# Seven block products instead of eight in the first halves of batches 3, 5 and 7, with the sums of the weight blocks placed anew

## The chip, the cores and the metric

The kernel runs on one core of one Trainium2 chip. The metric is the device time of one execution in microseconds (us). The core has five engines: TensorE (in the profile PE, with its weight loads as PEld), VectorE (DVE), ScalarE (ACT), GpSimd (POOL) and SyncE (SP), which here only starts DMAs. SBUF and PSUM are the core's two on-chip memories; in this kernel the products are written to PSUM, and VectorE and ScalarE read them there.

## The reference

```python
# attention between tokens x (8, 8, 512, 64) and states (8, 8, 32, 64)
xread = softmax(scale * x @ state.T) @ state         # per batch and head
sread = softmax(scale * state @ x.T) @ x
x = concat([xread, sread], axis=2)                   # -> (8 * 544, 512)
# mixture layer: w_in (512, 2048), w_out (2048, 512)
h = x @ w_in
return (h * cos(h)) @ w_out
```

All of it is float32. The kernel folds `state @ w_in` into a small matrix `sw` per batch, so that the first layer of a batch is a product with 256 rows to sum over (2048 x 256 by 256 x 512). It is made in 16 tiles of 128 x 512.

## The kernel before

A batch is 16 tiles. Two batches make a pair, and the second layer of a pair is made by Strassen's seven products already. So the 32 tiles of a pair fall into four phases of eight tiles: 0 and 1 are the two halves of the even batch, 2 and 3 those of the odd one. In phases 2 and 3 the gates are also subtracted from each other (`minus`).

The first layer of a tile is either plain, or it is made for two tiles together by Strassen's products. Plain is two matmuls of 512 columns a tile, four for two tiles. Strassen takes the 2 x 2 blocks of two tiles and needs seven products of 256 columns in place of eight:

```python
def hidden(t):                                   # plain: PE writes one of two PSUM buffers
    t.hp = hps.tile([P, S], F32, name="h")[:, 0:t.n]
    for i in range(t.kn):
        nc.tensor.matmul(out=t.hp, lhsT=t.lhs(i), rhs=t.rhs(i), ...)

def seven(t):                                    # which tiles go through seven products
    return t.pair is not None and t.b > 1 and t.phase < 2

def halves(b): ...    # four differences of 128 x 256 on VectorE, once a batch
def sw_sums(t):       # four sums of 128 x 128 weight blocks, once for two tiles
    ...
        nc.gpsimd.tensor_tensor(o, x1, x2, op=op)
def hidden_a(t, t2): ...   # four of the seven products, one copy on ScalarE
def sums_a(t): ...         # three sums on VectorE
def hidden_b(t): ...       # the other three products
def sums_b(t): ...         # two sums on VectorE
```

After that comes the gate h * cos(h), tile by tile, in four steps that alternate between ScalarE and VectorE:

```python
def gate(t):   nc.scalar.activation(t.q.bitcast(I32), t.hp, func=Copy, bias=0.25)
def gate2(t):  nc.vector.tensor_tensor(t.q, t.q.bitcast(I32), t.hp, op=subtract)
def gate3(t):  nc.scalar.activation(t.q, t.q, func=Sin, bias=halfpi, scale=-TWO_PI)
def gate4(t):  nc.vector.tensor_tensor(t.g, t.hp, t.q, op=mult)   # frees the PSUM buffer
```

Beside the tiles of a batch, the attention of the next batch is worked off by a plan of steps (one step is one tile, counted from 0, so step 8 is the ninth tile). In batches 3 and 5 it puts the scores into step 5 and the maxima, spreads, differences, exponentials, sums and the normalization into steps 5 to 9, most of them on VectorE. Finished results wait in a list (`later`), from which each step takes one: a total or a transpose on VectorE, with the store that follows it.

```python
        gate3(t)
        ...
        if later:
            later.pop(0)()
        for u in all_tiles[step + 3:step + 4]:       # sums for the first tiles of a pair
            if seven(u) and new_pair(u):
                sw_sums(u)
        gate4(t)
        ...
        if step in block_at:
            blocks(*block_at[step])                  # sums of w_out's blocks on GpSimd, once
        for u in all_tiles[step + 2:step + 3]:       # sums for the other tiles
            if seven(u) and u.f % 2 == 0 and not new_pair(u):
                sw_sums(u)
```

## Time and profile before

| | before |
|---|---|
| time, median | 769.69 us (768.45 to 770.36, 4 runs) |
| PE busy | 755.9 us, 98% of the span |
| DVE busy | 487.4 us, 63% |
| ACT, POOL busy | 314.1 us, 227.7 us |
| first layer, plain | 80 tiles |
| first layer, seven products | 24 pairs of tiles |

The prediction shows the lines. One note on reading them: an engine's share in the chain of work tells who was waited for, which is not the same as who was busy.

```profile
311.58 0.65 DVE L578 TENSOR_TENSOR g_all<-h,q 128x512 f32<-128x512 f32 x1
...
312.47 1.02 PE L471 MATMUL h<-aT,sw 128*128 128x512 f32 x2
```

### The profile page before, as it was taken

The page shows a single profiled execution, that of the slowest core. Times are in us where ns is not written, and L with a number is a line of the kernel's source. Part 1 is how long each engine was busy: PE and PEld are TensorE (multiplying, and loading weights), DVE is VectorE, ACT ScalarE, POOL GpSimd, SP SyncE. Part 2 cuts the span into 40 slices and gives each one's busy share as a digit, 9 for nine tenths or more (in the row PEclk, how much of TensorE's full clock was granted, in tenths as well). Part 3 has the DMA queues.
Part 4 walks back from the last instruction along what each step waited for, and adds up shares of the span by engine and source line. Part 5 has one row for each costly group of instructions (what it writes and reads, how often), then busy time and mean ns, then how long its engine had stood idle before and what let it go on. Part 6 is the DMA issues. An engine that isn't in the chain of part 4 may idle for free.

```text
span 768.0 us, 8094 instructions
## 1 busy us (share of the span) xinstructions
PE 755.9 (98%) x2808; PEld 367.0 (48%) x2808; DVE 487.4 (63%) x786; ACT 314.1 (41%) x511; POOL 227.7 (30%) x214
## 2 busy tenths in 40 slices
PE   8998999999999999999999999999999999999997
PEld 3443443444555434445555434455555444455554
DVE  5768777836896558847886558747876546431431
ACT  3887844532353325333362335333443333212112
POOL 2353278776120000653220001751210006500200
PEclk9999999999999999999999999999999999999999
DMA  8596461050012510340105210420100115000021
GB/s 246 170 275 212 127 95 28 7 104 1 10 18 45 93 28 0 55 84 0 27 2 98 41 27 15 76 47 0 28 1 14 22 21 137 0 1 14 15 41 41
DMA packets 161961, 43.52 MB, mean 57 GB/s; under 512 B 153921, under 2 KB 153921, under 8 KB 161921
## 3 DMA queue, kind: packets, MB, share of 16 engines
q1 hardware_dynamic: 161024, 42.49, 25.6%
q10 hardware_dynamic: 768, 0.39, 0.2%
q8 instruction: 22, 0.36, 0.2%
q0 software_dynamic: 128, 0.13, 0.1%
q14 instruction: 19, 0.15, 0.1%
HBM read 34.08 MB, written 8.91 MB: 56 GB/s over the span
## 4 chain that ended last, share of the span: by engine, by line
PE 91%; DVE 3%; POOL 2%; ACT 2%; DMA 1%; issue 1%; ACTq 0%; DVEq 0%; POOLq 0%
PE o L622 49%; PE h L471 20%; PE h L512 9%; PE at L319 4%; PE o L742 4%; PE at L409 2%; PE o L319 1%; POOL g_all L584 1%; PE at L392 1%; DMA g_all<-in_moe_w_in_dram 1%; DMA s<-in_state_dram 0%; POOL w_out L910 0%; DVE q L568 0%; ACT q L565 0%; DVE i L333 0%
## 5 line engine op out<-in xcount | busy, mean ns | idle before, releaser
L622 PE MATMUL o<-g_all,w_out 128*128 128x512 f32 x512 | 236.3, 598 | 0.4 <-POOL w_out L242 0.4
L584 POOL TENSOR_TENSOR g_all<-g_all 128x512 f32<-128x512 f32 x80 | 112.8, 1432 | 241.2 <-DVE g_all L578 241.2
L622 PE MATMUL o<-g_all,s 128*128 128x512 f32 x384 | 177.3, 598 | 0.0
L471 PE MATMUL h<-aT,sw 128*128 128x512 f32 x320 | 152.4, 599 | 2.9 <-DVE g_all L578 2.4
L568 DVE TENSOR_TENSOR q<-q,h 128x512 f32<-128x512 int32 (+1 forms) x93 | 59.4, 639 | 148.7 <-ACT q L565 148.6
L622 PEld LDWEIGHTS o<-g_all,w_out 128*128 128x128 f32 x512 | 93.8, 190 | 118.4 <-issue 114.6
L571 ACT ACTIVATE q<-q,halfpi 128x512 f32<-128x512 f32 (+1 forms) x144 | 100.7, 700 | 86.1 <-DVE q L568 85.9
L565 ACT ACTIVATE q<-h 128x512 int32<-128x512 f32 (+1 forms) x93 | 52.0, 559 | 204.3 <-PE h L471 204.1
L622 PEld LDWEIGHTS o<-g_all,s 128*128 128x128 f32 x384 | 70.8, 190 | 88.5 <-issue 86.5
L471 PEld LDWEIGHTS h<-aT,sw 128*128 128x128 f32 x320 | 60.7, 191 | 80.1 <-issue 67.3
L578 DVE TENSOR_TENSOR g_all<-h,q 128x512 f32<-128x512 f32 (+1 forms) x93 | 59.3, 637 | 35.0 <-ACT q L571 34.6
L565 ACT ACTIVATE q<-g_all 128x512 int32<-128x512 f32 x51 | 31.8, 624 | 90.9 <-DVE g_all L558 90.5
L568 DVE TENSOR_TENSOR q<-q,g_all 128x512 f32<-128x512 int32 x51 | 36.6, 717 | 28.6 <-ACT q L565 28.6
L242 POOL TENSOR_TENSOR w_out<-w_out,s 128x1024 int32<-128x1024 int32 x10 | 23.9, 2391 | 77.7 <-DVE w_out L237 71.5
L578 DVE TENSOR_TENSOR g_all<-g_all,q 128x512 f32<-128x512 f32 x51 | 37.0, 726 | 10.5 <-ACT q L571 10.4
L507 POOL TENSOR_TENSOR swS<-sw 128x128 f32<-128x128 f32 x24 | 11.4, 474 | 84.1 <-PE h L512 66.1
L584 DVE TENSOR_TENSOR g_all<-g_all 128x512 f32<-128x512 f32 x48 | 33.5, 697 | 1.6
L445 ACT COPY sw<-at 128x512 f32<-128x512 f32 x50 | 26.7, 586 | 10.8 <-PE at L319 10.4
L471 PE MATMUL h<-st_all,w_in 128*128 128x256 f32 x128 | 30.2, 379 | 0.0
L242 POOL TENSOR_TENSOR w_in<-w_in,s 128x1024 int32<-128x1024 int32 (+1 forms) x10 | 19.3, 1932 | 36.8 <-DVE w_in L237 34.6
L512 PE MATMUL h<-aS,swS 128*128 128x256 f32 x96 | 28.7, 380 | 1.0 <-POOL swS L507 1.0
L742 PE MATMUL o<-w_out,g_all 128*128 128x512 f32 x64 | 29.6, 592 | 0.0
(103 smaller groups left out, 785.3 us busy)
## 6 DMA issues: line engine op xcount, KB each, us to landing
out_dram<-ot SPq DMA_DIRECT2D x132, 64.0 KB, 2.0
g_all<-in_moe_w_out_dram SPq DMA_DIRECT2D x8, 1024.0 KB, 5.0
g_all<-in_moe_w_in_dram SPq DMA_DIRECT2D x6, 1024.0 KB, 5.4
xT<-in_x_dram SPq DMA_DIRECT2D x96, 64.0 KB, 2.3
x_b<-in_x_dram SPq DMA_DIRECT2D x24, 256.0 KB, 4.4
x_b<-in_x_dram SPq DMA_DIRECT2D x16, 128.0 KB, 3.9
g_all<-in_moe_w_in_dram SPq DMA_DIRECT2D x4, 512.0 KB, 5.8
x_b<-in_moe_w_out_dram SPq DMA_DIRECT2D x1, 1024.0 KB, 6.1
```

What stands on the lines that cost most here:

```text
L242: nc.gpsimd.tensor_tensor(bits, bits, e, op=ALU.add)
L319: nc.tensor.matmul(out=(to or at)[j][Ns * k:Ns * k + Ns, 0:n], lhsT=w[D * j:D * j + D, self.b, Ns * k:Ns * k + Ns], rhs=r(slice(D * j, D * ...
L445: (copy or nc.scalar.copy)(sw_of[self.b, nt][:, j, c0:c1], to[j][:, 0:c1 - c0])
L471: nc.tensor.matmul(out=t.hp, lhsT=t.lhs(i), rhs=t.rhs(i), start=(i == 0), stop=(i == t.kn - 1))
L512: nc.tensor.matmul(out=out, lhsT=w, rhs=r, start=True, stop=True)
L565: nc.scalar.activation(t.q.bitcast(I32), t.hp, func=ACTF.Copy, bias=0.25)
L568: nc.vector.tensor_tensor(t.q, t.q.bitcast(I32), t.hp, op=ALU.subtract)
L571: nc.scalar.activation(t.q, t.q, func=ACTF.Sin, bias=halfpi, scale=-TWO_PI)
L578: nc.vector.tensor_tensor(t.g, t.hp, t.q, op=ALU.mult)
L584: engine.tensor_tensor(out, a, b, op=ALU.subtract)
L622: nc.tensor.matmul(out=acc[bank][ch], lhsT=w[:, i, P * ch:P * ch + P], rhs=g.g, start=(i == 0), stop=(i == NH - 1))
L742: nc.tensor.matmul(out=acc[MAIN][i], lhsT=t.g[:, P * i:P * i + P], rhs=w_out[:, :, t.f, :], start=(t.n_th == 0), stop=(t.n_th == NF - 1))
```

## The change

It aims at TensorE: twelve more pairs of tiles go through seven products instead of eight. The sums of the weight blocks move forward in GpSimd's queue, and those for the very first pair go to VectorE. This is the whole diff, without the lines around it:

```diff
     def seven(t):
-        return t.pair is not None and t.b > 1 and t.phase < 2
+        return t.pair is not None and t.b > 1 and t.phase < 3
@@ sw_sums
+        engine = nc.vector if t.b < 2 or t.b == 2 and t.f == 0 else nc.gpsimd
         for o, x1, x2, op in (...):
-            nc.gpsimd.tensor_tensor(o, x1, x2, op=op)
+            engine.tensor_tensor(o, x1, x2, op=op)
@@ in each step, ahead of gate4
-        for u in all_tiles[step + 3:step + 4]:
-            if seven(u) and new_pair(u):
+        for u, new in zip(all_tiles[step + 2:step + 4], (False, True)):
+            if seven(u) and u.f % 2 == 0 and new_pair(u) == new:
                 sw_sums(u)
@@ in each step, behind the blocks of w_out
-        for u in all_tiles[step + 2:step + 3]:
-            if seven(u) and u.f % 2 == 0 and not new_pair(u):
-                sw_sums(u)
```

## The prediction

> **What bounds the kernel now.** I read the page first: the busy times of the engines, then the chain of work that ended last.
>
> ```profile
> span 768.0 us, 8094 instructions
> PE 755.9 (98%) x2808; PEld 367.0 (48%) x2808; DVE 487.4 (63%) x786; ACT 314.1 (41%) x511; POOL 227.7 (30%) x214
> ...
> PE 91%; DVE 3%; POOL 2%; ACT 2%; DMA 1%; issue 1%; ACTq 0%; DVEq 0%; POOLq 0%
> ```
>
> TensorE is busy for 98% of the span and makes 91% of the chain. The granted clock is 0.998. So a TensorE cycle that is saved is saved in the time, unless another engine then makes TensorE wait. Next come the groups by line, with the shapes apart, for the two ways of computing the first layer. L471 is the plain product. L512 is the Strassen product on half-width blocks.
>
> ```profile
> L471 PE MATMUL h<-aT,sw 128*128 128x512 f32 x320 | 152.4, 599 | 2.9 <-DVE g_all L578 2.4 <-ACT sw L445 0.5
> L512 PE MATMUL h<-aS,sw 128*128 128x256 f32 x96 | 28.9, 382 | 0.5 <-POOL sw L507 0.2 <-ACT g_all L955 0.2
> L512 PE MATMUL h<-aS,swS 128*128 128x256 f32 x96 | 28.7, 380 | 1.0 <-POOL swS L507 1.0
> L512 PE MATMUL h<-aT,sw 128*128 128x256 f32 x96 | 28.5, 379 | 0.0
> L512 PE MATMUL h<-aT,swS 128*128 128x256 f32 x48 | 14.7, 388 | 0.0
> ```
>
> Two things are to be seen. Every matmul in the source is two records: L471 has 320 records for 80 plain tiles with two matmuls each. L512 has 96+96+96+48 = 336 records for 24 pairs of tiles with seven matmuls each. And the mean durations (599 and 380 ns) contain the pipeline's depth, so they don't give the cost. The cost is the distance from one start to the next. I take it from the timeline and the chain: eight records of 512 columns stand there as 3.43 us, so 0.429 us each, and eight records of 256 columns as 1.73 us, so 0.216 us each.
>
> ```profile
> 350.02 1.73 PE h L512 x8
> 351.75 3.43 PE o L622 x8
> ```
>
> The third view is the busy time in stretches. The first line runs from the last Strassen products of batch 2 to the seventh tile of batch 3, so it is the first half of batch 3 less a tile. The second line is the rest of that batch. Columns: time, then busy time of PE, weight loads, DVE, ACT, POOL.
>
> ```profile
> 251.68:293.21 41.53, 41.53 (x139) 17.08 (x137) 24.49 (x38) 13.43 (x23) 0.00 (x0) 1.00 0.29 50
> 293.21:336.73 43.52, 43.52 (x162) 19.28 (x160) 32.57 (x51) 19.51 (x31) 20.05 (x17) 1.00 0.36 61
> ```
>
> In the stretch that the change converts, TensorE is full, VectorE is at 24.49 of 41.53 us and GpSimd does nothing at all. There is room for the sums there.
>
> **What the Trainium skill says.** "FP8 and Floating Point Precision", TensorE Precision Notes: true FP32 takes four passes through the array. "TensorE: Matmul & The Clock Gate", Back-to-back issue gap: a pass of N columns takes about N/2.4 + 2.5 ns, so 216 ns for 512 and 109 ns for 256. The trace agrees: two records of 429 ns are four passes of 215 ns, and two of 216 ns are four of 108 ns. Halving the width therefore costs almost nothing in efficiency, and 7/8 of the products is 7/8 of the time. "SBUF — State Buffer", Who interferes with whom: a DVE instruction with two SBUF inputs contends with a GpSimd instruction that reads SBUF, and the later one blocks. The trace agrees: L493, the differences of the halves, takes 411 ns at best but means of 1015 and 1074 ns where GpSimd's 1.43 us subtractions run beside it, and the sums of the weight blocks (L507) take 450 ns at best and up to 989 ns. The page on TensorE also has, under "Architectural detail", that GpSimd keeps strict order. That is what makes the place of the sums in its queue matter.
>
> **The change, part by part.**
>
> *(a) Products.* The first halves of batches 3, 5 and 7 are 3 x 8 tiles, so 12 pairs. A pair costs 8 records of 512 columns now, 8 x 0.429 = 3.43 us, and then 14 records of 256 columns, 14 x 0.2155 = 3.02 us. That is 0.42 us a pair and, times 12, -5.0 us, all of it on TensorE, the engine that sets the end. TensorE's records go from 2808 to 2808 - 12 x 2 = 2784.
>
> *(b) Sums on VectorE.* A pair adds three sums of 256 columns (415 to 421 ns, L542, L543, L557) and two of 512 (686 and 684 ns, L544, L558): 2.62 us; the gates then read SBUF instead of PSUM (717 to 726 against 682 to 684 ns), 0.04 x 4 = 0.15 us. Twelve pairs: +33 us of VectorE. Each odd batch adds four differences of halves (L493), at 0.41 us if GpSimd is quiet and up to 1 us if not: 1.7 to 4 us, three times. In the stretch shown, VectorE rises from 24.5 to 24.5 + 4 x 2.77 + about 2 = 37.6 us, of 41.5 - 1.7 = 39.8 us. That is 95%, but these stretches are run with three tiles of lag between the gate and the second layer, and the steps where VectorE has most (transposes, maxima) are followed by light ones.
>
> *(c) Copies and block sums.* ScalarE: 12 copies at 0.37 us = 4.4 us, on an engine that is 41% busy. GpSimd: 12 x 4 block sums at 0.45 us = 22 us, where it was idle. Both lie beside TensorE's work. The sums of a pair can start when the products of the pair before have been read, and have a step of about 5 us for 1.8 to 2.5 us of work.
>
> *(d) The sums placed anew.* Where batch 2 begins, GpSimd is late in the kernel before:
>
> ```profile
> 177.60 2.86 POOL L910 TENSOR_TENSOR w_out<-w_out 128x1024 f32<-128x1024 f32 x1
> ...
> 180.43 0.90 POOL L507 TENSOR_TENSOR swS<-sw 128x128 f32<-128x128 f32 x1
> ...
> 182.24 0.70 PE L512 MATMUL h<-aS,swS 128*128 128x256 f32 x2 [1.02 <-POOL swS L507]
> ...
> 183.18 0.70 PE L512 MATMUL h<-aS,sw 128*128 128x256 f32 x2 [0.24 <-POOL sw L507]
> ```
>
> The block subtraction of the second layer's weights (L910, 2.86 us) stands in the queue ahead of the sums for the second pair, and TensorE waits for them. From that pair's first product to the next group of products take 187.58 - 180.63 = 6.95 us here, and 355.02 - 349.86 = 5.16 us at the same place of batch 4, where no such subtraction runs: 1.8 us lost. After the change the sums stand before it, can start at 177.6 and end at about 179.6, before the products at 180.6. I count 1.6 us won, since batch 4 still shows 0.2 us of such a wait. The four sums for the first tile of batch 2 go to VectorE: 4 x about 0.3 us (an estimate from 0.415 us for 256 columns) in a stretch where it is 22.6 of 38 us busy. GpSimd sat idle before them for the same input (0.80 us for ScalarE's copy), so I give this part zero.
>
> *(e) New waits.* In the stretches that are Strassen already, starts are late by about 0.2 us where VectorE's sums come late: at the beginning of the second half of batch 4, and once more before its end. I take 0.2 us for each of the three new stretches, 0.6 us, and 0.1 us each for the halves, which have some 4 us from the last products of the old batch to the second product of the new: 0.3 us.
>
> Sum: -5.0 - 1.6 + 0.6 + 0.3 = -5.7 us. 769.6 - 5.7 = 763.9 us.
>
> **The rivals.**
>
> *VectorE becomes the bound in batches 3 and 5.* For it: the 95% of (b). Against: in the second half of batch 3, VectorE does 32.57 us of work in 43.52 us and TensorE never idles; in the first half of batch 4 it runs without a gap from 360 to 367 us and the products slip by 0.2 us. Batch 7 prepares no further batch (21.6 us of VectorE in its like stretch), so it is safe. If VectorE did bind, each of two stretches would lose 1 to 2 us: 766 to 768 us.
>
> *The halves or the block sums come late at the start of batches 3, 5, 7.* Both now run at the same moment, right after the last products of the even batch, on the two engines that block each other. Taken wholly in turn they need 4 x (0.41 + 0.45) = 3.4 us against about 4 us of TensorE work. If they miss, about 1 us each: 766 to 767 us.
>
> *The reordering gives nothing*, because GpSimd's backlog from the subtractions before it (L584, until 177.6) is the real limit. Against it: 1.02 and 0.24 us of wait are for L507 directly behind L910. Without this part: 765.5 us.
>
> **Range and chances.** 2% is 15.4 us. The whole saving is under half of that, and the rivals hardly make more than they take away. So "within 2%" is nearly certain. The low end, 762.2, is all of (a) and (d) with no new wait and a little more from (d); the high end, 767.3, is one rival in full.
>
> **What would show it.** Right: PE x2784; L512 at 336 + 168 = 504 records and L471 (512 columns) at 320 - 12 x 8 = 224; batch 3's first half shorter by about 1.7 us with POOL near 7 us; no wait on L507 behind L910 near 180 us, VectorE at about 527 us busy. Wrong: idle time before L512 that ends with VectorE's L493, L543, L544 or L558, or with L507, in the first halves of batches 3, 5 and 7; or a time above 767.3 us.

## More of the kernel before

The chain of work that ended last, before, at the place that matters later (start, length, what):

```profile
300.24 1.72 PE h L471 x4
301.95 1.72 PE o L622 x4
303.67 1.72 PE h L471 x4
305.39 1.02 PE at L319 x16
306.41 1.91 PE o L622 x4
308.32 1.72 PE h L471 x4
310.04 0.87 PE at L392 x8
310.91 1.72 PE o L622 x4
312.63 1.72 PE h L471 x4
```

These are the first tiles of the second half of batch 3. Every piece is PE's own work, end to end.

## The result

| | before | changed |
|---|---|---|
| time, median of 4 runs | 769.69 us | 765.75 us |
| ratio | | 0.9949 (0.9932 to 0.9966) |
| span of the profiled run | 768.0 us | 764.2 us |
| PE busy | 755.9 us | 751.7 us |
| DVE busy | 487.4 us | 520.3 us |
| POOL busy | 227.7 us | 249.3 us |

A ratio is the mean time of one kernel's fast runs over that of the other's of the same rounds, so it isn't quite the ratio of the medians. One kernel's runs scatter by 1 to 3 us. Part of that is a window at half clock, which shows in some profiles and not in others: from 74 to 77 us the granted clock was 0.50 in the changed kernel's profile (0.72 on average from 72 to 78 us, which makes about 3.4 us at half clock), and it was 1.00 throughout when the same kernel was run again (e11), and at the 13th tile of batch 1 the one was 1 us behind the other. So I use a sharper measure as well, the **stretch**: from the first product of the 13th tile of batch 1 (149.33 us before) to the first product of the state tiles at the end (670.99 us). All that the change touches lies between, and neither the start nor the end of the kernel does. The timelines give it (start, duration, engine, line, operation):

```profile
149.33 1.02 PE L471 MATMUL h<-aT,sw 128*128 128x512 f32 x2
...
670.99 1.24 PE L471 MATMUL h<-st_all,w_in 128*128 128x256 f32 x5
```

and the same two in the changed kernel:

```profile
149.28 1.02 PE L471 MATMUL h<-aT,sw 128*128 128x512 f32 x2
...
667.15 1.89 PE L471 MATMUL h<-st_all,w_in 128*128 128x256 f32 x8
```

That is 521.66 us before and 517.87 us after, 3.8 us less. A second profile of the changed kernel (e11) gave 517.87 us again, where the whole time doesn't repeat to 1 us. The kernel before was profiled once, so its 521.66 us has no such check of its own.

Now the page of the changed kernel, the lines that answer to those of the prediction:

```profile
PE 751.7 (98%) x2880; PEld 380.4 (50%) x2880; DVE 520.3 (68%) x862; ACT 316.3 (41%) x523; POOL 249.3 (33%) x258
...
PE 87%; DVE 7%; ACT 2%; issue 1%; DMA 1%; POOL 1%; SPq 0%; DVEq 0%; ACTq 0%; POOLq 0%
```

PE's share of the chain fell from 91 to 87%, and VectorE's rose from 3 to 7%. So some of the time is now spent waiting for VectorE. The chain in order of time shows where. It is the same place as shown above, the start of the second half of batch 3:

```profile
290.64 0.64 ACT q L567
...
291.30 0.69 DVE q L570
291.99 1.15 DVE xT L339
293.15 0.58 DVE g_all L580
...
296.25 1.21 DVE m L349 x2
...
299.28 1.43 ACT xT L365 x4
300.71 0.50 ACT q L567
...
303.67 0.65 DVE ot L651
304.32 0.59 DVE g_all L580
...
307.27 1.79 DVE aT L386
309.07 0.62 DVE ot L651
309.69 0.59 DVE g_all L580
...
310.32 1.98 PE h L471 x4
```

Where the chain before was PE's from end to end, for 20 us it is now VectorE's queue, with 3.6 us of ScalarE, mostly the exponentials (L360 and L365), in the middle. It ends in `gate4` (L580), which frees the PSUM buffer that the plain product of the twelfth tile (310.32) needs. The timeline names the waits:

```profile
304.95 1.98 PE L471 MATMUL h<-aT,sw 128*128 128x512 f32 x4 [0.18 <-DVE g_all L580]
310.32 1.98 PE L471 MATMUL h<-aT,sw 128*128 128x512 f32 x4 [0.79 <-DVE g_all L580]
```

The idle time in brackets is too small, since the modelled end of the record before runs into it. From start to start, the eleventh tile's product is 0.35 us late and the twelfth's 0.95 us, and the second record of each is 0.10 us late: 1.5 us. Batch 5 shows the same four numbers (0.34, 0.10, 0.95, 0.10), batch 7 none of them. Together that is 3.0 us. I call these the **late starts**. In the first halves of batches 3, 5 and 7 themselves, the part that the change converts, no new wait is to be found.

The other end of the change worked. GpSimd now does the sums (L509) ahead of the block subtraction (L912), and the products at 180.5 us follow one another without a wait:

```profile
177.67 0.91 POOL L509 TENSOR_TENSOR swS<-sw 128x128 f32<-128x128 f32 x1
...
180.52 0.59 PE L514 MATMUL h<-aT,sw 128*128 128x256 f32 x2
180.89 4.68 POOL L912 TENSOR_TENSOR w_out<-w_out 128x1024 f32<-128x1024 f32 x2
180.95 0.59 PE L514 MATMUL h<-aS,swS 128*128 128x256 f32 x2
```

My theory was then: -1.9 us from the placing, -5.0 us from the products, +3.0 us from the late starts, which makes -3.9 us, and 3.8 us were measured. The rivals: that the placing causes the late starts; that GpSimd's subtractions beside VectorE do; or that every Strassen pair simply yields less than reckoned.

### The profile page after: what moved, and what is told of

It is laid out like the page before. It is cut to its first block, busy times and chain, and to the rows that moved or that the text cites. A ratio compares the mean times of both kernels' runs of the same rounds, so it can differ in the third digit from the quotient of the medians.

```text
span 764.2 us, 8416 instructions
## 1 busy us (share of the span) xinstructions
PE 751.7 (98%) x2880; PEld 380.4 (50%) x2880; DVE 520.3 (68%) x862; ACT 316.3 (41%) x523; POOL 249.3 (33%) x258
## 4 chain that ended last, share of the span: by engine, by line
PE 87%; DVE 7%; ACT 2%; issue 1%; DMA 1%; POOL 1%; SPq 0%; DVEq 0%; ACTq 0%; POOLq 0%
PE o L624 47%; PE h L514 14%; PE h L471 14%; PE at L319 4%; PE o L744 4%; PE at L409 2%; DVE xT L339 1%; PE o L319 1%; DVE q L570 1%; DVE g_all L580 1%; DVE i L333 1%; DMA g_all<-in_moe_w_in_dram 1%; ACT q L567 1%; PE at L392 1%; DVE aT L356 1%
## 5 line engine op out<-in xcount | busy, mean ns | idle before, releaser
L586 POOL TENSOR_TENSOR g_all<-g_all 128x512 f32<-128x512 f32 x80 | 112.8, 1433 | 121.2 <-DVE g_all L580 121.2
L570 DVE TENSOR_TENSOR q<-q,h 128x512 f32<-128x512 int32 (+1 forms) x69 | 42.9, 621 | 103.6 <-ACT q L567 103.6
L471 PE MATMUL h<-aT,sw 128*128 128x512 f32 x224 | 107.2, 602 | 4.8 <-DVE g_all L580 4.3
L567 ACT ACTIVATE q<-g_all 128x512 int32<-128x512 f32 x75 | 46.8, 624 | 141.8 <-DVE g_all L560 141.4
L567 ACT ACTIVATE q<-h 128x512 int32<-128x512 f32 (+1 forms) x69 | 37.6, 545 | 131.0 <-PE h L471 131.0
L570 DVE TENSOR_TENSOR q<-q,g_all 128x512 f32<-128x512 int32 x75 | 52.7, 703 | 35.5 <-ACT q L567 35.5
L471 PEld LDWEIGHTS h<-aT,sw 128*128 128x128 f32 x224 | 41.8, 190 | 60.2 <-issue 45.0
L509 POOL TENSOR_TENSOR swS<-sw 128x128 f32<-128x128 f32 x35 | 17.4, 496 | 148.6 <-PE h L514 107.3
L580 DVE TENSOR_TENSOR g_all<-g_all,q 128x512 f32<-128x512 f32 x75 | 54.0, 720 | 14.5 <-ACT q L573 14.4
L580 DVE TENSOR_TENSOR g_all<-h,q 128x512 f32<-128x512 f32 (+1 forms) x69 | 42.8, 621 | 23.5 <-ACT q L573 23.1
L509 POOL TENSOR_TENSOR swS<-sw,swS 128x128 f32<-128x128 f32 x35 | 18.3, 522 | 87.4 <-PE h L514 86.9
L514 PE MATMUL h<-aS,sw 128*128 128x256 f32 x144 | 43.1, 381 | 0.1
L514 PE MATMUL h<-aT,sw 128*128 128x256 f32 x144 | 42.8, 379 | 0.0
L586 DVE TENSOR_TENSOR g_all<-g_all 128x512 f32<-128x512 f32 x48 | 33.5, 697 | 1.6
```

The costliest lines, as they stand in the source:

```text
L471: nc.tensor.matmul(out=t.hp, lhsT=t.lhs(i), rhs=t.rhs(i), start=(i == 0), stop=(i == t.kn - 1))
L509: engine.tensor_tensor(o, x1, x2, op=op)
L514: nc.tensor.matmul(out=out, lhsT=w, rhs=r, start=True, stop=True)
L567: nc.scalar.activation(t.q.bitcast(I32), t.hp, func=ACTF.Copy, bias=0.25)
L570: nc.vector.tensor_tensor(t.q, t.q.bitcast(I32), t.hp, op=ALU.subtract)
L580: nc.vector.tensor_tensor(t.g, t.hp, t.q, op=ALU.mult)
```

## The experiments

Eleven runs were made, each of five rounds in turn with the kernel before (4 to 6 times were taken of each; each was profiled once). "Stretch" is the measure above as a difference from the 521.66 us of before; "late starts" are those of batches 3 and 5 together.

| run | stretch | late starts | time, median | ratio to before (95%) |
|---|---|---|---|---|
| changed | -3.80 us | 3.0 us | 765.75 | 0.9949 (0.9932 to 0.9966) |
| e1 placing only | -1.87 | none | 766.86 | 0.9969 (0.9957 to 0.9982) |
| e2 products only | -1.94 | 3.0 | 766.98 | 0.9970 (0.9957 to 0.9983) |
| e3 batch 7 only | -3.51 | none | 766.2 | 0.9959 (0.9946 to 0.9973) |
| e4 attention later (wrong result) | -0.42 | elsewhere | 768.3 | 0.9994 (0.9976 to 1.0012) |
| e5 transposes later | -6.19 | 0.6 | 763.59 | 0.9916 (0.9902 to 0.9929) |
| e6 differences on GpSimd | -1.99 | others | 767.98 | 0.9969 (0.9956 to 0.9982) |
| e7 four tiles | -3.67 | others | 765.15 | 0.9942 (0.9929 to 0.9956) |
| e8 e5 and e6 together | -4.37 | others | 765.14 | 0.9937 (0.9924 to 0.9949) |
| e9 idle work | -3.81 | 3.0 | 765.71 | 0.9952 (0.9939 to 0.9965) |
| e10 plain, transposes later | -1.83 | none | 767.68 | 0.9973 (0.9960 to 0.9986) |
| e11 changed again | -3.79 | 3.0 | 765.21 | 0.9948 (0.9934 to 0.9962) |

### The parts of the change alone: e1, e2, e3

e1 takes the changed kernel and leaves the odd batches plain:

```diff
-        return t.pair is not None and t.b > 1 and t.phase < 3
+        return t.pair is not None and t.b > 1 and t.phase < 2
```

> The sums of the weight blocks stand where the change puts them, but the odd batches stay plain. Theory (the changed kernel's gain is -1.9 us from the placing, -5.0 us from the products, +3.0 us from VectorE's late gates in batches 3 and 5): 769.7 - 1.9 = 767.8 us, with no wait on the block subtraction near 180 us. Rival (the placing is worth little, and the products were worth only 4 us): 769 us or more.

The stretch was 1.87 us shorter, and the waits near 180 us were gone. The placing is worth what the theory says and makes no late starts. The median was under the forecast; the times of that session were lower as a whole (the kernel before had 768.97 us in it).

e2 takes the kernel before and changes only `t.phase < 2` to `t.phase < 3`, so that the sums stay where they were.

> The odd batches' first halves go through the seven products, but the sums stay at their old places and all on GpSimd. Theory: 769.7 - 5.0 + 3.0 = 767.7 us, with the same two late starts of the plain product in the second halves of batches 3 and 5 (0.35 and 0.95 us, and 0.1 each behind them). Rival (the new placing itself makes the late starts): about 764.7 us and no late starts there.

The late starts were 0.33 and 0.95 us in both batches, as in the changed kernel, and the wait on the block subtraction was there as in the kernel before. So the products alone make the late starts. The parts add up: -1.87 - 1.94 = -3.81 us, and the whole change has -3.80.

e3 takes the changed kernel with the odd half converted in batch 7 alone:

```diff
-        return t.pair is not None and t.b > 1 and t.phase < 3
+        return t.pair is not None and t.b > 1 and t.phase < 2 + (t.b == B - 1)
```

> New placing, and of the odd batches only batch 7 goes through the seven products. It prepares no further batch, so VectorE has little else to do. Theory: 769.7 - 1.9 - 1.7 = 766.1 us, no late start in batch 7; batches 3 and 5 together would then be worth only 0.3 us of the 3.3 us that their products save. Rival (each batch loses alike): 767.8 - 0.7 = 767.1 us.

The four pairs of batch 7 give 3.51 - 1.87 = 1.64 us, against 4 x 0.42 = 1.68 us reckoned. The eight pairs of batches 3 and 5 give 3.80 - 3.51 = 0.29 us, where 3.4 us were reckoned. A pair does yield what was reckoned, and two batches lose nearly all of it.

### Moving the attention: e4, a failed experiment

```diff
+                d = int(b in (3, 5))
                 early(b + 1, (1 + (b == 1), 2 + (b == 1),
-                              5, 6, 7, 8, 9))
-                late(b + 1, (10, 11, 12, 15))
+                              5 + d, 6 + d, 7 + d, 8 + d, 9 + d))
+                late(b + 1, (10 + d, 11 + d, 12 + d, 15))
```

> The changed kernel, with the attention work of batches 4 and 6, done in batches 3 and 5, one tile later from the scores on (maxima, spreads, differences, exponentials, sums, turns), so that less of it falls on the last two Strassen pairs. Theory (VectorE's clump of work in tiles 5 to 9 makes the second half start late): the late starts fall from 1.5 us a batch to under 0.7, 764.0 us or less. Rival (not the clump but GpSimd's subtractions beside VectorE in the second half hold it up): they start at the same tiles as before, so the late starts stay, 765.8 us or more.

The result was wrong, by my own edit: with one step more, the second part of the reads falls into step 13, where the plan also makes the weight products of the next batch in the same PSUM buffers, and those are overwritten between the two parts of the reads. That is read from the code, not shown by a run of its own. The times don't help either. A product (L319) that needs those buffers now started 1.99 us late in each of the two batches, behind the exponentials that had moved next to it. The run tells nothing about the theory.

### Shortening VectorE's queue: e5

In the stretch of chain shown above stand two transposes of finished results (L651, at 303.67 and 309.07 us). Nobody is in a hurry for them. In e5, steps 8 and 9 of batches 3 and 5 take nothing from the list of finished results, so these come two steps later:

```diff
-        if later:
+        if later and not (t.b in (3, 5) and s in (8, 9)):
             later.pop(0)()
```

> The changed kernel, but in the first two tiles of the second halves of batches 3 and 5 the two waiting transposes of results (0.65 us each on VectorE) are put off by two tiles. Nothing else changes. Theory (the late starts come from VectorE's own queue, which is full from the last Strassen pair to the gate that frees the buffer): the chain is about 1.2 us shorter, the late starts fall from 1.5 us a batch to about 0.3, and the time is 2.4 us under the changed kernel's, 6.3 us under that of the kernel before. Rival (GpSimd holds VectorE up, or ScalarE's exponentials set the pace): the late starts stay, 3.9 us under the kernel before.

The stretch went from -3.80 to -6.19 us. That is 2.39 us for four transposes, 0.60 us each, which is the distance from their start to the start of the next VectorE operation in the changed kernel's timeline (0.58 and 0.63 us for the two of batch 3), and less than their records' durations (0.65 and 0.70 us). The time was 763.59 us, ratio 0.9916. The same two products, in e5's timeline:

```profile
303.24 1.88 PE L471 MATMUL h<-aT,sw 128*128 128x512 f32 x4
...
307.75 1.55 PE L471 MATMUL h<-aT,sw 128*128 128x512 f32 x3
```

The timeline names no wait before either of them. From start to start the second is still 0.20 us late and its second record 0.10 us, in both batches: 0.3 us a batch, as forecast. This version beats both kernels; the interval of its ratio (0.9902 to 0.9929) lies just below that of the changed kernel (0.9932 to 0.9966, and 0.9934 to 0.9962 in e11).

### Was it the queue's length? e9, e10, e11

e9 is e5 with other work of about the same length where the transposes were:

```diff
+        if t.b in (3, 5) and s in (8, 9):
+            idle = small.tile([P, 1], F32, name="idle")
+            nc.vector.tensor_reduce(out=idle, in_=w_in[:, 0, 0:S], op=ALU.max,
+                                    axis=AX.X)
```

> The kernel with the transposes put off, and in their old places two reductions of 128 x 512 elements whose result nobody reads (about 0.6 us of VectorE's queue each, one SBUF input). Theory (only the length of VectorE's queue counts): the late starts come back, about 0.35 and 0.95 us in batches 3 and 5, 3.8 us under the kernel before. Rival (the transposes themselves matter, by the buffer that they free or the stores that they start): no late starts, 6.2 us under it.

The late starts were back, 0.33 and 0.95 us, and the stretch was -3.81 us, as in the changed kernel. It is neither the stores nor the buffers that the transposes free, but the time that they take in VectorE's queue.

e10 is e5 with `t.phase < 2`, so with plain odd batches.

> The odd batches plain, the new placing, and the transposes put off. Theory (without the sums of the Strassen products VectorE's queue is not what TensorE waits for): nothing beyond the placing, 1.9 us under the kernel before. Rival (putting the transposes off is a gain of its own, 2.4 us with any products): 4.3 us under it.

It gave -1.83 us, the placing alone (e1: -1.87). Putting the transposes off is worth nothing without the Strassen products and 2.4 us with them. So it is the conversion that uses up VectorE's slack. It does two things at once, and no run parts them: it makes TensorE come earlier, and it puts sums into VectorE's queue. That the sums matter is read from the timelines: ahead of `gate2` of the seventh and eighth tile of batch 3 VectorE idles 1.44 and 0.80 us in the kernel before, 1.44 and 0.81 us in e10, and 0.76 us and not at all in the changed kernel.

> The changed kernel once more, beside the two runs above on the same chip. Every theory: 3.8 to 3.9 us under the kernel before, late starts of 0.35 and 0.95 us in batches 3 and 5.

-3.79 us, with late starts of 0.34 and 0.95 us.

### Taking the work elsewhere: e6 and e8

GpSimd has little to do in the first halves, so e6 gives it the differences of the gates there in batches 3 and 5 (`soon` is what sends them to VectorE):

```diff
         if t.phase == 2:
-            minus(pr, pr.b[0, i].g, t.g, pr.b[0, i].g, True)
+            minus(pr, pr.b[0, i].g, t.g, pr.b[0, i].g, t.b == B - 1)
```

> The changed kernel, but the differences of the gates in the first halves of batches 3 and 5 go to GpSimd, which is idle there (1.43 us each in place of 0.69 on VectorE). Theory: VectorE loses 3 x 0.6 us of work between the last Strassen pair and the late starts, and the late starts fall to under 0.7 us a batch, about 5.5 us under the kernel before. Rival (what VectorE gains it loses again by waiting for GpSimd, since the gates of Strassen tiles read two operands from SBUF): late starts stay or grow, the gate operations of these tiles last longer than 0.73 us on average, and the time is 3.9 us or less under the kernel before.

It was worse than the changed kernel by 1.8 us, and the reason isn't quite the one that I wrote down for the rival. The gate operations of these tiles hardly got longer (0.67 to 0.70 us on average, against 0.67 to 0.69). What got longer are the differences of the second half, which are still on VectorE. In the changed kernel (timeline, L586):

```profile
304.93 0.69 DVE L586 TENSOR_TENSOR g_all<-g_all 128x512 f32<-128x512 f32 x1
304.98 3.01 POOL L586 TENSOR_TENSOR g_all<-g_all 128x512 f32<-128x512 f32 x2 [24.64 <-DVE g_all L580]
```

and in e6:

```profile
304.62 1.27 POOL L586 TENSOR_TENSOR g_all<-g_all 128x512 f32<-128x512 f32 x1 [5.37 <-DVE g_all L580]
304.64 1.79 DVE L586 TENSOR_TENSOR g_all<-g_all 128x512 f32<-128x512 f32 x1
```

Both engines subtract at the same moment, each with two operands in SBUF. In the changed kernel VectorE is 0.05 us ahead, takes 0.69 us, and GpSimd waits. In e6 VectorE comes 0.02 us after GpSimd and takes 1.79 us, and so at the first four tiles of the half (at one of them, in batch 5, 1.44 us). Why it comes later I can only argue: its operand now comes from GpSimd, so it has one more semaphore to wait for. With that, one product started 1.35 us late, and another, which waits for VectorE to empty a PSUM buffer, 0.85 us, in each batch.

These traces also answer in part the rival that GpSimd's subtractions beside VectorE make the late starts. The normalization (L386), just ahead of the gate that the twelfth tile waits for, takes 1.79 us in batches 3 and 5 of the changed kernel, beside a subtraction of GpSimd's, and 1.20 us in e6, where none runs beside it. So about 0.6 us of that queue is GpSimd's doing. But it was 1.79 us in the kernel before as well: it is part of what left so little slack, and not what the change added.

> The transposes put off and the differences on GpSimd, together. Theory: no late starts over 0.2 us, so the whole -1.9 and -5.0 us: 6.7 us under the kernel before. Rival (contention with GpSimd): slower than with the transposes put off alone.

The two edits together gave -4.37 us, less than the transposes alone (-6.19). The late product of the twelfth tile was all but gone (0.16 us), and the 0.85 us wait stayed.

### Converting half: e7

```diff
-        return t.pair is not None and t.b > 1 and t.phase < 3
+        return t.pair is not None and t.b > 1 and (
+            t.phase < 2 or t.phase == 2 and (t.b == B - 1 or t.f < 4))
```

> Of the odd batches' first halves only the first four tiles go through the seven products in batches 3 and 5, all eight in batch 7. Theory: the last two pairs cost VectorE more than they save TensorE. No late starts, and 1.9 + 1.7 + 4 x 0.42 = 5.2 us under the kernel before. Rival (any Strassen pair in batches 3 and 5 is lost again later): 3.5 us under it, as with batch 7 alone.

The number is the rival's (-3.67 us, with batch 7 alone -3.51), but not because the late starts came back. Of those there are none. Instead a product of the second layer now starts 0.64 us late in each of the two batches:

```profile
274.58 1.98 PE L625 MATMUL o<-g_all,s 128*128 128x512 f32 x4 [0.48 <-DVE held L631]
```

It waits for VectorE to take the result of the phase before out of PSUM (L631), and that stood behind transposes for the attention. With the record behind it, 0.10 us late, that makes 0.74 us a batch, and both batches together the 1.5 us that are missing from the forecast. In the changed kernel no wait for VectorE over 0.2 us shows in this half. So converting fewer tiles only moved the place where TensorE meets VectorE's queue.

## Why the prediction was right or wrong

The time, 765.75 us, lies in the range (762.2 to 767.3). The change stayed within 2% of the kernel before, as was nearly certain. Predicted were -5.7 us, measured -3.9. That the time lies in the range is in part luck: 3.0 us of waits came that the sum did not have, 0.9 us of waits that it had did not come, and the placing gave 0.3 us more.

- **(a) Products: right, with a slip in the count.** 0.42 us a pair were predicted, and batch 7 measured 1.64 us for four. The record count was wrong: the text says 2784, but eight records give way to fourteen, so 2808 + 12 x 6 = 2880, which is what the page shows. The prediction's own counts of 504 and 224 agree with that.
- **(b), (c) Work on the other engines: right, except for the forecast of busy time.** By durations of records, the twelve pairs' sums took 31.3 us (31.4 reckoned), the twelve new differences of halves 5.1 us (0.42 us each, the quiet end of what was reckoned), the first weight sums on VectorE 1.2 us, and the gates nothing (1.8 reckoned). ScalarE's copies took 4.5 us. The page's busy time rose by less, 32.9 us for VectorE where the prediction had about 40, since neighbouring records overlap by 0.08 us and busy time counts that once. GpSimd's rose by 21.6 us, against 22. The stretch of batch 3 for which the prediction had 39.8 us and VectorE 95% busy took 39.89 us (249.77 to 289.66 us), with VectorE at 33.57 us, 84%, and GpSimd at 6.77 us.
- **(d) Placing: right in mechanism, a little small.** 1.6 us predicted, 1.87 measured (e1). The sums for the second pair started at 177.67 us as foreseen, but ended at 180.93 us and not at 179.6, since three of the four took 0.87 to 0.91 us; no product waited for them.
- **(e) New waits: this step failed.** It took 0.2 us for each of the three new first halves and 0.1 us for each set of halves, 0.9 us in all. There were none of these, and 3.0 us somewhere else: at the third and fourth tile of the second halves of batches 3 and 5. The step looked for waits where the change adds work. But what stands in VectorE's queue ahead of a gate delays it (e5, e9), and TensorE's plain products take two PSUM buffers in turn; the delay is carried along the queue until a buffer isn't free in time. It comes to light after the Strassen tiles end, among the sums, the spread and the normalization of the next batch's attention.
- **The first rival** named the engine and the size (1 to 2 us in each of two batches), and batch 7 as safe. All that held. But none of the prediction's signs of being wrong would have shown it: they look for idle time before the Strassen products (L512) in the first halves, and the waits fell on plain products in the second. The argument against the rival did not hold: it read the share of busy time of VectorE in a whole half, and a place in batch 4 where VectorE runs without a gap and TensorE is hardly late. What mattered was the slack at one point. In the kernel before, the gate of the tenth tile ended at 312.23 us, and the product that needs its buffer started at 312.47: 0.24 us to spare. In the changed kernel TensorE comes to the ninth tile 3.56 us earlier than before (296.52 against 300.08), of which 1.87 are the placing and 1.7 the four pairs. VectorE starts that gate operation 1.96 us earlier (309.62 against 311.58), so by hardly more than the placing. TensorE's lead of 1.6 us less the 0.24 is 1.4 us, about the 1.5 of the late starts. The number to read off was in the profile before. Not tested is ScalarE's part of the chain: VectorE waits 1.06 us for it at the ninth tile, in the kernel before as in the changed one, and e4, which moved the exponentials, came out wrong.
- **The second rival** (sums late at the start of the odd batches) didn't happen: no wait for L509 or L493 shows in their first halves.
- **The third rival** (the reordering gives nothing) is refuted by e1.

## What to carry to other kernels

When the bound engine gets faster, look for the places at which another engine's in-order queue has the least slack behind it, measured as the time between the release of a buffer and its use; those come up next, and they need not lie where the change adds work. Work that nobody waits for, such as the transposes of finished results, should stand outside such a stretch of the queue: here that one condition was worth 2.4 us, more than half as much as the change itself. And handing work to an idle engine isn't free where the two can block each other.

## What the Trainium skill lacked or had wrong

- "SBUF — State Buffer", Who interferes with whom, has that the first of the two engines to issue keeps the shared reads. The trace agrees, and e6 adds how fine it is: 0.02 us behind GpSimd cost VectorE 1.1 us (1.79 in place of 0.69), 0.05 us ahead of it cost VectorE nothing (GpSimd's subtraction then took 1.77 in place of 1.27).
- "TensorE: Matmul & The Clock Gate", Back-to-back issue gap, gives N/2.4 + 2.5 ns, but for an isolated matmul, and says that in a stream it over-counts at 512 columns (about 216 ns against 131 measured), which the prediction left out. For the float32 passes here the page's caveat does not hold, and the formula nearly does: from start to start, in a stream, a pass is 214.7 ns for 512 columns (half of 429.3) and 107.9 for 256 (half of 215.8), against 215.8 and 109.2. No page that I found says that a float32 matmul stands in the profile as two records, each two passes long, so that there are twice as many records as matmuls (320 for 160 in L471).
